# Two pairs of weight pieces in flight, three normalisations on GpSimd, and a new order, in a four-layer transformer kernel

## The chip, the cores and the metric

The kernel runs on one core of a Trainium2 chip. The metric is device time in microseconds (us); lower is better. A core has five engines that run on their own and meet through semaphores: TensorE (PE, matrix products), VectorE (DVE, elementwise work), ScalarE (ACT, activations and copies), GpSimd (POOL, elementwise work at a slower pace) and SyncE (SP, which here only issues DMAs). DMAs move data between HBM, the on-chip memory SBUF and, as transposes, within SBUF. Products land in PSUM, which has 8 banks.

## What is computed

Four layers on x of 2048 tokens by 448, in bfloat16. Layers 0 and 2 are attention over a short dilated window, layers 1 and 3 are a gated product (here called FFN):

```
x = x + A(layernorm(x), wqkv, wo)          # layer 0
x = x + B(layernorm(x), w_gate, w_up, w_down)   # layer 1
x = x + A(layernorm(x), wqkv, wo)          # layer 2
x = x + B(layernorm(x), w_gate, w_up, w_down)   # layer 3

A: 16 heads of 28; each token looks at itself and the 7 tokens at distances 2, 4, ... 14 before it;
   logits = q.k * 28**-0.5, softmax over the 8 places, weighted sum of v, then times wo (448 x 448)
B: ((x @ w_gate) * (x @ w_up)) @ w_down     # 448 -> 1792 -> 448, no activation function
```

The same weights serve layers 0 and 2, and layers 1 and 3.

## The kernel before

**Tiling.** Tokens lie in 16 blocks of 128. A layer is worked in chunks of 256 or 512 tokens, named by layer and number: A00 to A04, B10 to B14, A20 to A23, B30 to B34. `SEQ` gives the order in which the chunks are described, and chunks of neighbouring layers overlap: B10 can run once the first blocks of layer 0 are finished. Nearly every product uses half of the 128 rows of the PE array, so two matmuls run side by side ("a pair").

**A block's way through attention.** `ln_chunk` makes the layer norm: bn_stats and bn_aggr on DVE (the rows with `st` and `mv`), two small ACT operations (`lnv`, `rstd`), and the normalisation proper, a `tensor_scalar` into `xn_sb` (L788), on DVE. In layer 0 the block is then transposed on PE (`Tps`, L798 and L802) and copied to `xnTa` (L809, L812) by ACT or DVE; later layers transpose by DMA (L791, issued by SP). `qk_chunk` makes queries and keys (products with `WQK`, copy to `qk` at L898), `v_group` the values (products with `WV`). Attention goes by nine groups of up to two query blocks. For a group, `attn_front` masks the queries (`Qz`, DVE, L1009), multiplies them with the keys in 64 small matmuls (S, L1021), takes the exponent on ACT (L1030) and applies the window mask on DVE (L1037); `attn_back` multiplies with the values in 64 small matmuls (AV, L1055), collects the result in `O_sb` (L1066, L1070), and `norm` divides by the softmax sum (L1080 to L1093). `y_blocks` multiplies by `wo_g` and adds into `x_sb` (L1110).

**FFN.** `b_chunk` has 14 units; a unit is seven pairs with `WGU` (gate and up weights side by side), a copy of the gate half by ACT (`g_sb`, L1146) and a product on DVE into `hT` (L1149). Four pieces of `WD` then make the output, in two parts: the first needs units 0 to 6, the second units 7 to 13.

**What sets the order.** All operations are handed to a list scheduler inside the kernel (`Sched`). It steps through a planned time with an estimate for each operation, takes on each engine the ready operation of lowest priority number, and writes the resulting fixed order for each engine. Priorities are the sum of a base, `PR` by kind, `JP` by chunk and `XP` by operation number; these tables hold tuned numbers. The small matmuls of S and AV ("bursts") are joined up to `JOIN` at a time, and a burst can take in the first steps of a waiting product, split into strips of 32 columns (L538, the "host"). The planner also models that PE's instructions arrive in lines: `LINE = 254` instructions, the first boundary moved by `LINE_0 = 62`; a line's delay is a constant by time (6.5, 5.5 or 3.9 us).

**Weights.** The input `x` and the attention weights are loaded first. Then SP issues, each step waiting for the one before to land: the four pieces of `wo_g`; the first pair (gate and up piece); and so on through six pairs (two halves of the columns, three parts of the rows, `KPARTS`), and the four pieces of `WD`, one at a time. So one pair is in flight. The write of ones into the scratch tensor `vt` stands behind `wo_g`. SP also issues the writes of value pieces to `vt` (L907), their transposed reads (L918), and the output; its queue is in order.

## Time and profile before

| | |
|---|---|
| time, median of 3 runs | 391.83 us (389.53 to 392.62) |
| profiled execution: its own time | 391.56 us |
| its span, first to last instruction | 389.6 us |
| PE busy | 380.8 us, 6565 matmuls |
| DVE busy | 287.0 us |
| ACT busy | 209.0 us |
| POOL busy | 7.8 us |
| TensorE clock granted, mean | 0.996 |

The page gives each engine's busy time and a row of 40 slices (9.74 us each) with tenths of busy time. PE looks full almost everywhere, but a busy PE is not PE at its peak: ends of matmuls are modelled, so short waits between matmuls vanish in that row. The starts are sharp, and the prediction goes by them. A group row reads: line, engine, operation, output and inputs, shapes, count, then busy us and mean ns of one, then idle time before them and what ended it. A timeline row reads: start, duration (both us), then the same, with the idle time and its releaser in brackets.

### The profile page before, as it was taken

How to read it: one execution, taken by the hardware profiler on the slowest of the kernel's cores; microseconds unless marked ns; L12 is line 12 of the kernel's file. 1: busy time of each engine (PE TensorE's matmuls, PEld its weight loads, DVE VectorE, ACT ScalarE, POOL GpSimd, SP SyncE). 2: the span in 40 equal slices, each digit the busy share in tenths (PEclk: the TensorE clock that was granted, in tenths of full speed). 3: DMA queues.
4: the chain of work that ended last, by engine and by line, in shares of the span. 5: the costliest groups of instructions: out<-in, count | busy, mean ns of one | idle time of the engine just before them, and what ended most of it. 6: DMA issues, size and time to landing. Idle time of an engine off the chain costs nothing.

```text
span 389.6 us, 14816 instructions
## 1 busy us (share of the span) xinstructions
PE 380.8 (98%) x6565; PEld 214.7 (55%) x6565; DVE 287.0 (74%) x638; ACT 209.0 (54%) x393; POOL 7.8 (2%) x37
## 2 busy tenths in 40 slices
PE   8989989899999999999999999999999999999997
PEld 3646558455555544454766557654555444544584
DVE  6998989599968975399656997575967994376343
ACT  4887865397455775246454455565634842263140
POOL 6010000000000000000000000000000000000000
PEclk9989999999999999999999999999999999999999
DMA  8543574710711313004113132310133042100201
GB/s 276 161 106 76 137 101 124 122 23 9 87 25 34 47 39 56 10 6 86 21 22 50 30 63 37 75 32 2 27 54 96 3 47 52 48 2 3 60 14 49
DMA packets 54867, 22.53 MB, mean 58 GB/s; under 512 B 44996, under 2 KB 54804, under 8 KB 54804
## 3 DMA queue, kind: packets, MB, share of 16 engines
q1 hardware_dynamic: 54372, 21.08, 27.4%
q8 instruction: 52, 0.85, 0.9%
q10 hardware_dynamic: 432, 0.52, 0.5%
q14 instruction: 11, 0.09, 0.1%
HBM read 8.54 MB, written 2.71 MB: 29 GB/s over the span
## 4 chain that ended last, share of the span: by engine, by line
PE 93%; ACT 3%; DMA 1%; issue 1%; DVE 1%; SPq 0%; ACTq 0%
PE ps L535 82%; PE ps L538 3%; PE ps L1055 2%; PE ps L1021 2%; PE ps L697 2%; ACT E_sb L1030 1%; PE ps L1161 1%; DMA WD<-in_B_w_down_dram 1%; ACT xnTa L812 1%; ACT qk L898 1%; ACT g_sb L1146 0%; ACT xnTa L809 0%; DVE x_sb L1110 0%; PE ps L802 0%; DVE hT L1149 0%
## 5 line engine op out<-in xcount | busy, mean ns | idle before, releaser
L535 PE MATMUL ps<-xnTb,WGU 64*128 64x512 bf16 (+1 forms) x1908 | 174.4, 332 | 0.2
L535 PEld LDWEIGHTS ps<-xnTb,WGU 64*128 64x128 bf16 x1908 | 92.6, 94 | 67.8 <-issue 1.1
L1146 ACT ACTIVATE g_sb<-ps 128x512 bf16<-128x512 f32 (+1 forms) x140 | 71.1, 511 | 87.8 <-PE ps L535 71.7
L1149 DVE TENSOR_TENSOR hT<-g_sb,ps 128x512 bf16<-128x512 bf16 (+1 forms) x140 | 79.6, 576 | 43.1 <-ACT g_sb L1146 40.7
L535 PE MATMUL ps<-WD,hT 64*128 64x448 bf16 x778 | 78.6, 349 | 1.5 <-DMA WD<-in_B_w_down_dram 1.4
L535 PEld LDWEIGHTS ps<-WD,hT 64*128 64x128 bf16 x778 | 36.9, 94 | 36.0 <-issue 1.7
L535 PE MATMUL ps<-xnTa,WQK 64*128 64x512 bf16 (+1 forms) x492 | 55.2, 360 | 0.5 <-ACT E_sb L1030 0.3
L1110 DVE TENSOR_TENSOR x_sb<-x_sb,ps 128x448 bf16<-128x448 bf16 x62 | 36.4, 615 | 23.3 <-PE ps L535 23.3
L1030 ACT ACTIVATE E_sb<-ps,shift_sb 128x1024 bf16<-128x1024 f32 (+1 forms) x36 | 36.8, 1073 | 24.5 <-PE ps L1021 24.4
L767 DVE BATCH_NORM_STATS2 st<-x_sb 128x6 f32<-128x448 bf16 x64 | 37.7, 612 | 0.2
L788 DVE TENSOR_SCALAR xn_sb<-x_sb,mv,rstd 128x896 bf16<-128x896 bf16 (+1 forms) x64 | 34.7, 568 | 2.7 <-ACT rstd L772 2.5
L535 PEld LDWEIGHTS ps<-xnTa,WQK 64*128 64x128 bf16 x492 | 23.9, 96 | 22.2 <-issue 1.5
L898 ACT ACTIVATE qk<-ps 128x1024 bf16<-128x1024 f32 (+1 forms) x26 | 24.6, 956 | 11.3 <-PE ps L535 11.2
L535 PE MATMUL ps<-wo_g,oT 64*128 64x448 bf16 x256 | 29.1, 349 | 0.1
L1037 DVE TENSOR_TENSOR E_sb<-E_sb,MK 128x1024 bf16<-128x1024 bf16 (+1 forms) x36 | 23.6, 661 | 6.8 <-ACT E_sb L1030 6.5
L1081 ACT ACTIVATE R_sb<-R_sb 128x480 f32<-128x480 f32 (+1 forms) x34 | 20.5, 603 | 11.1 <-DVE R_sb L1080 10.6
L535 PE MATMUL ps<-WV,xnTa 64*128 64x336 bf16 (+3 forms) x248 | 23.1, 304 | 0.0
L1080 DVE STREAM_SHUFFLE R_sb<-O_sb 128x480 f32<-128x480 f32 (+1 forms) x34 | 23.1, 696 | 0.0
L1093 DVE TENSOR_TENSOR oT<-O_sb,R_sb 128x480 bf16<-128x480 f32 (+3 forms) x36 | 22.0, 624 | 0.8 <-ACT R_sb L1082 0.6
L1009 DVE TENSOR_SCALAR Qz<-qk,qmask 128x960 bf16<-128x960 bf16 (+1 forms) x36 | 14.7, 451 | 9.2 <-PE ps L1021 8.0
L1082 ACT ACTIVATE R_sb<-R_sb 128x480 f32<-128x480 f32 (+1 forms) x34 | 20.0, 600 | 0.3
L535 PEld LDWEIGHTS ps<-wo_g,oT 64*128 64x128 bf16 x256 | 12.4, 94 | 12.4 <-DVE oT L1093 0.9
(64 smaller groups left out, 231.6 us busy)
## 6 DMA issues: line engine op xcount, KB each, us to landing
out_dram<-x_sb SPq DMA_DIRECT2D x15, 112.0 KB, 1.7
x_sb<-in_A_x_dram SPq DMA_DIRECT2D x3, 448.0 KB, 6.0
WGU<-in_B_w_gate_dram SPq DMA_DIRECT2D x4, 224.0 KB, 3.6
WGU<-in_B_w_up_dram SPq DMA_DIRECT2D x4, 224.0 KB, 3.9
WD<-in_B_w_down_dram SPq DMA_DIRECT2D x2, 448.0 KB, 4.0
WGU<-in_B_w_gate_dram SPq DMA_DIRECT2D x2, 336.0 KB, 4.5
WGU<-in_B_w_up_dram SPq DMA_DIRECT2D x2, 336.0 KB, 6.3
vt<-qk SPq DMA_DIRECT2D x42, 16.0 KB
```

The costliest lines, as they stand in the source:

```text
L535: return lambda E: E.matmul(out(), lhs(), rhs(), start=start, stop=stop)
L767: sc.add("dve", one(lambda E, B=B: E.bn_stats(st6[:, B, :], x_sb[:, B, :]), ("bn", li, B)), 525.0, deps=[("x", li - 1, B)] + ([("xn", li - ...
L788: sc.add("dve", one(lambda E, B=B, dst=dst, src=src: E.tensor_scalar(dst, src, mv[:, B, 0:1], rstd[:, B:B + 1], ALU.subtract, ALU.mult), ( ...
L898: return E.activation(dst, src, ACT.Copy) if hasattr(E, "activation") else E.tensor_copy(dst, src)
L1030: return E.activation(E_sb[:, slot, 2 * hp:2 * hp + 2, 0:w], ps[:, b0:b0 + 2, 0:w], ACT.Exp, bias=shift_sb[:, 0:1], scale=SCALE)
L1037: return E.tensor_tensor(e, e, MK[:, kind, 0:nc].unsqueeze(1).unsqueeze(1).to_broadcast([128, 2, w // nc, nc]), ALU.min)
L1080: sc.add("dve", one(lambda E: E.stream_shuffle(R_sb[:, rs, 0:w], O_sb[:, os_, 0:w], [DH] * 32), ("Rs", li, qb)), dve_est(w) + 20.0, deps=[ ...
L1081: sc.add("act", one(lambda E: E.activation(R_sb[:, rs, 0:w], R_sb[:, rs, 0:w], ACT.Ln), ("Rl", li, qb)), act_est(w, False), deps=[("Rs", l ...
L1093: return E.tensor_tensor(oT[:, :, a % HALF:a % HALF + z - a], O[:, :, a - tok:z - tok], R_sb[:, rs, 0:w].rearrange("p (h n) -> p h n", h=4 ...
L1110: sc.add("dve", one(lambda E: E.tensor_tensor(x_sb[:, B, :], x_sb[:, B, :], ps[:, bk[w], 0:D], ALU.add), ("x", li, B)), dve_est(D), deps=[ ...
L1146: sc.add("act", one(lambda E, gs=gs, bk=bk: E.activation(g_sb[:, gs, 0:nt], ps[:, bk[0], 0:nt], ACT.Copy), ("G", li, j, fc)), act_est(nt), ...
L1149: sc.add("dve", one(lambda E, gs=gs, bk=bk, fc=fc: E.tensor_tensor(hT[:, fc, hs, 0:nt], g_sb[:, gs, 0:nt], ps[:, bk[1], 0:nt], ALU.mult), ...
```

## The change

1. **Weight loads.** A list `gates` replaces the single gate. Each pair waits for the pair two steps back, so two pairs are in flight; the first two wait for parts of `x`. `wo_g` moves from ahead of the first pair to behind the first half (three pairs); the write of ones waits for a piece of the second half. The `WD` pieces wait two steps back as well. Each piece gets a semaphore of its own.
2. **Normalisation.** In layer 0 the planner may place the normalisation of blocks 3 to 9 on POOL, at a planned 2,250 ns; the planned DVE time in FFN layers goes from 540 to 645 ns.
3. **Planner.** The delay of an instruction line follows from the DMAs that are in flight (`line_at`) instead of constants; bursts are no longer joined (`JOIN` 3 to 1); caps, holds and all priority tables are new.
4. **The order that results.** On POOL the normalisations of blocks 3, 7 and 9 stand behind the mask building. On PE, all four first query-and-key units run ahead of the first values; five attention groups (before: four) and more of `wo` stand ahead of the first FFN product. All weight issues stand on SP ahead of the first write to `vt`. PE has 18 S and 18 AV bursts, each on its own, in 36 stretches (before: 33). The matmuls are the same, but for a few that are split into strips in other places (6559 instructions in place of 6565).

```
-JOIN = 3
+JOIN = 1
...
-HOLD_A = 5940.0
-HOLD_BA = 13780.0
-HOLD_BB = 680.0
-HOLD_N = 2
+HOLD_A = 12410.0
+HOLD_BA = 40320.0
+HOLD_BB = 12030.0
+HOLD_N = 1
...
-ATT_P = 3.0
+ATT_P = 1.0
 A_CAP = 5
-B_CAP = 6
+B_CAP = 8
...
+    def line_at(self, at):
+
+        t = at + self.LINE_A
+        for issued, landed in self.moves:
+            if issued <= at + self.LINE_B:
+                t = max(t, landed - self.LINE_B)
+        return t + self.LINE_C
...
-            self.lines.append(at + (self.LINE_H if at < self.HEAD_T else self.LINE_W if at < self.HEAD_W else self.LINE_T))
+            self.lines.append(self.line_at(at))
...
-    plain_dma("sp", ones_dst, ones_src, ("vones",), "d_one", deps=["c_ones"] + [("wo", j) for j in range(4)], lat=4000.0, prio=-44.5)
-    for j in range(4):
-        dst = wo_g[32 * j:32 * j + DH, :, :]
-        src = A_wo.rearrange("(c j e) d -> j e c d", c=4, j=4, e=DH)[j]
-        plain_dma("sp", dst, src, ("wo", j), "d_wo", deps=["c_wo", ("x", -1, 11)], lat=3600.0, prio=-45)
-    gate = [("wo", j) for j in range(4)]
+    plain_dma("sp", ones_dst, ones_src, ("vones",), "d_one", deps=["c_ones", ("wu", 1, 0)], lat=6000.0, prio=-44)
+    gates = [[("x", -1, 11)], [("x", -1, 15)]]
     for n in range(2):
         f0, f1 = F // 2 * n, F // 2 * (n + 1)
         for i, (a, z) in enumerate(KPARTS):
             for w, lo, src in (("wg", 0, B_w_gate), ("wu", 64, B_w_up)):
-                plain_dma("sp", WGU[lo:lo + 64, a:z, f0:f1], ..., f"d_{w}{n}", deps=gate, ..., mode=i)
-            gate = [("wg", n, i), ("wu", n, i)]
+                plain_dma("sp", WGU[lo:lo + 64, a:z, f0:f1], ..., f"d_{w}{n}{i}", deps=gates[-2], ..., est=650.0)
+            gates.append([("wg", n, i), ("wu", n, i)])
+        if n == 0:
+            for j in range(4):
...
+                plain_dma("sp", dst, src, ("wo", j), "d_wo", deps=["c_wo"] + gates[-2], lat=4000.0, prio=-44)
+            gates[-1] = gates[-1] + [("wo", j) for j in range(4)]
     for n in range(FC // 7 * 2):
         a, z = 7 * n // 2, 7 * (n + 1) // 2
-        plain_dma("sp", WD[:, a:z, :], ..., ("wd", n), f"d_wd{n // 2}", deps=gate, ..., mode=n % 2)
-        gate = [("wd", n)]
+        plain_dma("sp", WD[:, a:z, :], ..., ("wd", n), f"d_wd{n}", deps=gates[-2], lat=4200.0, prio=-44)
+        gates.append([("wd", n)])
...
-            sc.add("dve", one(lambda E, ...: E.tensor_scalar(dst, src, mv[:, B, 0:1], rstd[:, B:B + 1], ALU.subtract, ALU.mult), ("xn", li, B)),
-                   325.0 if par == 0 else 540.0, ...)
+            sc.add(("dve", "pool") if li == 0 and 3 <= B < 10 else "dve", one(lambda E, ...: E.tensor_scalar(...), ("xn", li, B)),
+                   {"dve": 325.0 if par == 0 else 645.0, "pool": 2250.0}, ...)
```

The tables `PR`, `JP`, `XP` and `HEAD_P`, which are new throughout, are left out.

More of the change, by code (lines that the diff above doesn't have):

```diff
@@ L36 @@
 HEAD_LN = 5
-HEAD_P = (-7243.45, -6839.28, 6873.65, 2231.18, -2220.8)
-HOLD_A = 5940.0
-HOLD_BA = 13780.0
-HOLD_BB = 680.0
-HOLD_N = 2
+HEAD_P = (-13350.35, -12608.87, 4149.99, 4834.42, -5790.0)
+HOLD_A = 12410.0
+HOLD_BA = 40320.0
+HOLD_BB = 12030.0
+HOLD_N = 1
 AV_EST = 288.0
@@ L58 @@
 NBK = 8
-PR = {'Qz': 1078.85, 'AV': -4851.85, 'rstd': -1339.07, 'bn': 4568.65, 'N': -1817.78, 'Gps': 8610.65, 'Tps': -31.38, 'H': -4889.6, 'S': 2643.48, 'VT': 544.99, 'Ex': 596.45, 'G': -2837.24, 'xn': -3500.95, 'QK': 2639.1, 'Ddps': 940.66, 'V': 567.07, 'x': -8.65, 'lnv': 5266.82, 'Oc': 2625.17, 'Oa': 3443.2, 'R': -727.31, 'VVps': -3592.23, 'Yps': -11164.33, 'PW': 3164.05, 'T': -1396.37, 'mv': -2211.6, 'Rs': 1799.38, 'Rl': -488.18, 'QKps': 1399.61, 'E': 778.94, 'wqk': 1537.92, 'wqp': 1028.96}
@@ L61 @@
-JP = {'A20': -25.69, 'B32': -196.33, 'B34': -5191.89, 'A22': -98.13, 'B13': 6648.45, 'A21': -2562.96, 'B12': 1135.93, 'A02': 1939.91, 'A03': 1924.97, 'B30': 4558.29, 'B31': -653.55, 'B10': -3350.57, 'B11': -1722.9, 'A23': -7569.63, 'A04': -2325.27, 'B33': 4017.0, 'A01': -2467.87, 'B14': -3725.84, 'A00': -900.45}
+PR = {'Qz': 4799.43, 'AV': -4782.7, 'rstd': -6066.81, 'bn': 10063.34, 'N': 913.74, 'Gps': 11694.76, 'Tps': -4880.31, 'H': -10872.83, 'S': 203.36, 'VT': 66.35, 'Ex': 2432.38, 'G': -8403.33, 'xn': -4241.77, 'QK': 746.33, 'Ddps': 1807.32, 'V': -1125.57, 'x': 232.06, 'lnv': 8673.99, 'Oc': 2256.02, 'Oa': 3868.14, 'R': -6136.18, 'VVps': -2694.46, 'Yps': -13771.91, 'PW': 5680.47, 'T': -1301.17, 'mv': -7586.23, 'Rs': 1454.22, 'Rl': 1876.37, 'QKps': 398.71, 'E': -1505.89, 'wqk': 3921.06, 'wqp': 1513.4}
@@ L62 @@
+JP = {'A20': 2129.71, 'B32': 145.71, 'B34': -8865.09, 'A22': -1908.07, 'B13': 6929.64, 'A21': -3873.02, 'B12': -320.7, 'A02': 4273.6, 'A03': 6346.7, 'B30': 6263.14, 'B31': 805.07, 'B10': -3539.76, 'B11': -146.0, 'A23': -11058.38, 'A04': -7082.55, 'B33': 8155.41, 'A01': -2596.71, 'B14': -5692.45, 'A00': 5097.12}
 LOAD_L = 2000.0
@@ L147 @@
     LINE_0 = 62
-    LINE_T = 3900.0
-    LINE_H = 6500.0
-    HEAD_T = 14000.0
-    LINE_W = 5500.0
-    HEAD_W = 46000.0
+    LINE_A = 1200.0
+    LINE_B = 1100.0
+    LINE_C = 2700.0
     def __init__(self):
@@ L276, in schedule @@
         self.pe_done = []
+        self.moves = []
         ndep, users = {}, {}
@@ L419, in schedule @@
                     free[e] = op.end
+                    if op.dma is not None:
+                        self.moves = self.moves[-39:] + [(op.end, max(op.end + op.lat, op.land))]
                 order[e].append((got, seq))
@@ L612, in build @@
     sem_names = ["pe", "act", "dve", "pool"]
-    sem_names += [f"d_x{i}" for i in range(NCH)] + ["d_stg0", "d_stg1", "d_stg2", "d_stg3", "d_wv", "d_wo", "d_wg0", "d_wg1", "d_wu0", "d_wu1", "d_wd0", "d_wd1", "d_out", "d_out2"]
+    sem_names += [f"d_x{i}" for i in range(NCH)] + ["d_stg0", "d_stg1", "d_stg2", "d_stg3", "d_wv", "d_wo", *[f"d_{w}{n}{i}" for w in ("wg", "wu") for n in range(2) for i in range(len(KPARTS))], *[f"d_wd{n}" for n in range(4)], "d_out", "d_out2"]
     sem_names += ["d_x0h"]
@@ L625, in act_table_load, with plain_dma @@
         return E.add_instruction(atl)
-    def plain_dma(q, dst, src, key, sem, deps=(), lat=LOAD_L, prio=0.0, tmin=None, mode=0):
-        sc.add(q, one(lambda E: E.dma_start(dst, src), key), {"sp": 520.0, "act": 500.0, "pool": 1000.0}[q], deps=deps, dma=sem, mode=mode, lat=lat, land=LAND.get(sem[2:], 0.0), prio=prio, tmin=tmin)
+    def plain_dma(q, dst, src, key, sem, deps=(), lat=LOAD_L, prio=0.0, tmin=None, est=None):
+        sc.add(q, one(lambda E: E.dma_start(dst, src), key), est or {"sp": 520.0, "act": 500.0, "pool": 1000.0}[q], deps=deps, dma=sem, mode=0, lat=lat, land=LAND.get(sem[2:], 0.0), prio=prio, tmin=tmin)
     CH_ROWS = [0, 128, 192, 320]
@@ L729, in build @@
             for w, lo, src in (("wg", 0, B_w_gate), ("wu", 64, B_w_up)):
-                plain_dma("sp", WGU[lo:lo + 64, a:z, f0:f1], src[64 * a:64 * z, f0:f1].rearrange("(k p) f -> p k f", p=64), (w, n, i), f"d_{w}{n}", deps=gate, lat=LOAD_L + 224 * (z - a) / RATE, prio=-44, mode=i)
-            gate = [("wg", n, i), ("wu", n, i)]
+                plain_dma("sp", WGU[lo:lo + 64, a:z, f0:f1], src[64 * a:64 * z, f0:f1].rearrange("(k p) f -> p k f", p=64), (w, n, i), f"d_{w}{n}{i}", deps=gates[-2], lat=1900.0 + 1000.0 * (z - a), prio=-44, est=650.0)
+            gates.append([("wg", n, i), ("wu", n, i)])
+        if n == 0:
+            for j in range(4):
+                dst = wo_g[32 * j:32 * j + DH, :, :]
+                src = A_wo.rearrange("(c j e) d -> j e c d", c=4, j=4, e=DH)[j]
+                plain_dma("sp", dst, src, ("wo", j), "d_wo", deps=["c_wo"] + gates[-2], lat=4000.0, prio=-44)
+            gates[-1] = gates[-1] + [("wo", j) for j in range(4)]
     for n in range(FC // 7 * 2):
         a, z = 7 * n // 2, 7 * (n + 1) // 2
-        plain_dma("sp", WD[:, a:z, :], B_w_down[128 * a:128 * z, :].rearrange("(c p) e -> p c e", p=128), ("wd", n), f"d_wd{n // 2}", deps=gate, lat=LOAD_L + 112 * (z - a) / RATE, prio=-44, mode=n % 2)
-        gate = [("wd", n)]
+        plain_dma("sp", WD[:, a:z, :], B_w_down[128 * a:128 * z, :].rearrange("(c p) e -> p c e", p=128), ("wd", n), f"d_wd{n}", deps=gates[-2], lat=4200.0, prio=-44)
+        gates.append([("wd", n)])
     WDR = [("wd", n) for n in range(4)]
@@ L787, in ln_chunk @@
             nt = 4 if par == 0 else 7
-            sc.add("dve", one(lambda E, B=B, dst=dst, src=src: E.tensor_scalar(dst, src, mv[:, B, 0:1], rstd[:, B:B + 1], ALU.subtract, ALU.mult), ("xn", li, B)),
-                   325.0 if par == 0 else 540.0, deps=[("rstd", li, B), ("mv", li, B), ("x", li - 1, B), prev], prio=prio - 0.2)
+            sc.add(("dve", "pool") if li == 0 and 3 <= B < 10 else "dve", one(lambda E, B=B, dst=dst, src=src: E.tensor_scalar(dst, src, mv[:, B, 0:1], rstd[:, B:B + 1], ALU.subtract, ALU.mult), ("xn", li, B)),
+                   {"dve": 325.0 if par == 0 else 645.0, "pool": 2250.0}, deps=[("rstd", li, B), ("mv", li, B), ("x", li - 1, B), prev], prio=prio - 0.2)
             if not by_pe:
```

2 lines of the change are left out of this document (1 added, 1 removed).

## The prediction

> **What bounds the kernel now.** First the busy row of the page, then stretches of 10 us, then the waits of PE.
>
> ```profile
> PE 380.8 (98%) x6565; PEld 214.7 (55%) x6565; DVE 287.0 (74%) x638; ACT 209.0 (54%) x393; POOL 7.8 (2%) x37
> ```
>
> PE is full. What its matmuls need at least follows from the starts in the timeline, where a stretch without a wait stands:
>
> ```profile
> 15.90 3.84 PE L535 MATMUL ps<-xnTa,WQK 64*128 64x512 bf16 x34
> ```
>
> 34 matmuls are 17 pairs; the last takes .16 beyond its start distance, so (3.84 - .16)/17 = .216 us a pair of 512 columns. Likewise .189 for 448, .143 for 336, .109 for 256. Summed over all matmuls this is **361.4 us**, for the new order too, since the products are the same. So 391.56 (the profiled execution) = 1.95 outside the span + 1.3 to the first matmul + 361.4 + 24.2 of lost time between + 2.8 behind the last. Only the 24.2 can move. I call the sum of prices ahead of a matmul its *position*, and the wall time less the position its *lag*. Before, the lag is 4.7 us at position 17.3, 7.4 at 18.6, 9.8 at 24.1, 13.4 at 42.2 (first FFN product, wall 55.6), 15.5 at 59.0 (wall 74.5), 25.5 at the end. So two thirds are lost in the first 75 us, where layer 0 starts:
>
> ```profile
> 20.00:30.00 10.00, 8.33 (x193) 4.90 (x191) 8.49 (x23) 8.43 (x18) 1.03 (x5) 0.83 0.46 111
> 40.00:50.00 10.00, 8.81 (x188) 4.45 (x182) 8.71 (x21) 8.52 (x14) 0.00 (x0) 1.00 0.63 124
> 90.00:100.00 10.00, 10.00 (x100) 4.64 (x96) 9.80 (x20) 5.76 (x11) 0.00 (x0) 1.00 0.06 13
> ```
>
> The columns are the stretch, its length, busy us of PE, weight loads, DVE, ACT, POOL, then the granted clock. In the first, the clock is .83: it was .5 for 3.41 us (26.64 to 30.05), after PE had lost .92, .79 and .48 us to DVE and ACT within 23.8 to 26.1. In both early rows DVE has 85% and more. Named stalls are few:
>
> ```profile
> PE ps L535 <- DMA WD<-in_B_w_down_dram: 1.4, 1, 1.4
> PE ps L1021 <- issue: 1.2, 1, 1.2
> ...
> 50.03 0.47 PE L1021 MATMUL ps<-Qz,qk 64*32 64x80 bf16 x38 [1.22 <-issue]
> 70.48 1.50 PE L535 MATMUL ps<-WD,hT 64*128 64x448 bf16 x14 [1.41 <-DMA WD<-in_B_w_down_dram]
> ```
>
> The first is the output weights, landed at 70.4, two us after the last `hT` of the first FFN chunk (68.43). The second is an instruction wait in the middle of an S burst. The instruction queue shows why:
>
> ```profile
> q8 instruction: 52, 0.85, 0.9%
> ...
> q8 instruction: 1, 0.02, 1.1%
> ```
>
> 52 packets of 16 KB serve 13,130 PE instructions, one per 252 (126 matmuls and their loads). Each leaves .2 to 4.0 us (mean 1.7) after PE passed the boundary before it, takes .9 to 1.45, and the waiting matmul started 1.6 us behind the packet's end. The second row is the stretch 43 to 50: PE passed the boundary at 43.24, the packet went at 47.2, in transfers that fill the queues, and the matmul ran at 50.03, **6.8 us** later. Unloaded it would be 1.7 + 1.15 + 1.6 = 4.5. A line covers 126 matmuls: some 13 us of wide products, but little more than 1 us of small ones.
>
> **The change, part by part.**
>
> *Weights two pairs at a time.* A pair took 4.65 us from issue to next issue (16.37, 21.03, 25.68), some 2 of them in transfer. All weights are 5.1 MB; with two in flight at 448 KB in 2 us they need 23 us, so the last `WD` piece lands near 38 in place of 70.4 if the first pair goes at 15. The 1.41 us wait at 70.48 (1.58 between the matmuls) goes. What is late next is the last `hT`, so the gain exists only if DVE gets there sooner. `wo_g` behind the first half must be there at its first product, position 30.1, about wall 42. All weight issues now stand on SP ahead of the first `vt` write, which went at 38.9 before; the last of them goes when the `WD` piece two back has landed, some 4 us before the end, at 34, so the writes behind it are not held (bounds 0 and +2, if the loads run a third slower). Gain: 0 to 1.6, inside the sum below.
>
> *Normalisation on POOL.* Three operations of .323 us (start to start) leave DVE, .97 in all. The trace has no such operation on POOL. Its rows there: a copy of 448 in 558 ns, a two-input product of 72 in 356 ns; by the first an operation costs .6 us, by the second, scaled by size, 2.5. I take the diff's 2.25, close to the upper row; POOL was idle for 14.1 us ahead of 22.77, so three in a row (6.75 us) hide there. Bounds: -1.0 us, and +1.3 if the last one is bare (2.25 - .97).
>
> *The order, to position 18.9.* Two of the three moved normalisations precede the waits at 23.8 to 26.1, which end on DVE: .65 off, lag 7.4 - .65 = 6.8, position 18.85 at 25.6. I leave out a half clock here.
>
> *Position 22.9 to 24.1.* From there to position 22.9 the lag grew by some .5 outside the half clock: wall 30.2. In the new order a line ends at 22.9 (in the fourth S burst) and the next at 24.0 (in the second AV burst): 1.1 us of streaming, while the smallest distance before was 1.4. The line called at 30.2 comes after 4.5 to 6.8 us, and at that time two weight pairs are under way. I take the middle, 5.6: position 24.05 at 35.8. PE is then idle 4.5 us, and the clock was .5 where a 3.41 us stretch had 35% of PE activity, and whole at 51%; a half clock that covers 1.2 us of the streaming behind costs .6 (bounds 0 and 1.7, the latter half of 3.41). Lag 12.4, against 9.8.
>
> *To the end of the first FFN chunk.* The new order has one more attention group ahead of the first FFN product (position 45.4, was 42.2). DVE's work from the same place to the last `hT` is, priced by start-to-start distances of its rows (.605 for an `hT` of 512, .32 of 256, .536 bn, .56 norm product, .588 shuffle, and so on), **35.9 us**. Before, from 33.8 to 68.43 it did 29.9 us of such work in 34.6: 86%. Part of its idle time was the instruction wait and PE's own lateness, which are paid already here, so I take midway to full, 93%: 38.6 us, and 35.8 + .6 + 38.6 = 75.0 for position 59.0. PE alone would be there sooner: 36.4 + 34.9 + 5 bursts of .35 (the rate of late bursts, below) = 73.0. The lag is 16.0, before 15.5: **+.5**. Both old stalls are gone, and the new line wait with the longer head gives it back.
>
> *The rest.* From position 59 the lag grew by 10.0, with 26 S and AV stretches at about .35 each as the main part. The new order has 26 there as well; FFN is fed by the same weights. Line boundaries stand 4.1 us apart or more, at the closest 3.0 before, which may save one late line of 1; more bursts stand alone, which may cost as much. I take 0, bounds -1 and +1.
>
> Sum: 391.56 + .5 = **392.1 us**, beside the median of 391.83.
>
> **Weighing a rule.** POOL beside DVE is what decides the second part. In the trace:
>
> ```profile
> 22.77 1.03 POOL L713 COPY WQK<-hT 128x64 bf16<-128x64 bf16 x5 [14.11 <-PE ps L535]
> ...
> 22.96 0.40 DVE L788 TENSOR_SCALAR xn_sb<-x_sb,mv,rstd 128x512 bf16<-128x512 bf16 x1
> ```
>
> The normalisation ran inside POOL's copies in .40 us, its usual 403 ns. So no block shows, though POOL's copies are short. The Trainium skill's page "SBUF — State Buffer", section "Who interferes with whom", says otherwise: DVE and GpSimd share a port pair, DVE's copies and `tensor_scalar` in their two-port modes take it whole, and the one who comes second fully blocks. The row here speaks against it as far as it reaches; the last rival below is what it would give.
>
> **Rivals.**
>
> 1. *The forecast*: gains and losses cancel, 392.1. Chance .45.
> 2. *The head packs tightly.* Fetches come at 4.5 us with no half clock (24.05 at 34.7) and DVE is full (35.9, 70.6); then PE's own 34.9 + 1.75 ends last, at 71.4, lag 12.4: -3.1, **388.4**. For it: weights done by 38 leave the queues empty in 40 to 70; against: DVE never ran at 100% in the head. A line in 3 us (the fastest delay, .2 + 1.15 + 1.6) gives 387. Chance .25, of which .15 beyond 1%.
> 3. *Slower by lines behind weights.* Two pairs in flight hold the call at 30.2 for 6.8 us (37.0), the idle PE brings the half clock (1.7), and DVE runs at 86% (41.7): 80.4, lag 21.4, +5.9: **397.5**. It decides from a delay of about 6.5 us. For it: the 6.8 of before stood in full transfers. Against: at most one pair may still be moving. Chance .17.
> 4. *Slower by POOL beside DVE.* If every copy, normalisation and two-input product of DVE that starts during POOL's 6.75 us waits for its end, some three quarters of DVE's work there, 5 us, come late; a little idle takes 1: **396**. Chance .08.
> 5. *The loads gain nothing*: two pairs share the transfers, the weights land no earlier, and the wait of 1.6 stays behind the last `hT`: 392.1 + 1.6 = **393.7**. Chance .05.
>
> About 1% (3.9 us) is what a measurement of this kernel tells from no change. Faster by more: .15 (out of 2). Slower by more: .28 (3, most of 4, and a tail of 1 and 5). Within: .57. The range runs from 387.2 (2 with a quick line) to 397.5 (3).
>
> **What will show it.** Right: no wait for `WD`; last `WD` landed before 45; a PE gap of some 4.5 us near matmul 600 (the second AV burst); three normalisations on POOL of about 2.2 us and DVE at its usual durations beside them; lag 14 to 16 at the first FFN chunk's end; 10 us of loss behind. Wrong: no gap at that line (2), a gap over 5.5 with .5 clock (3), DVE starts held until POOL's ends (4), or losses behind 75 us that are not 10, which I have only carried over.

## The result, and the profile after

The changed kernel takes **392.69 us** (median of 20 runs, 388.5 to 395.15), against 389.81 for the kernel before in the 20 runs beside it: 2.9 us or .7% between the medians. Over fast runs alone (within 1.5% of a kernel's fastest, which leaves out three of the changed kernel's) the ratio is 1.0044, 95% interval 1.0023 to 1.0065. Either way it is slower by less than the 1% that the prediction called no change, and the median is .6 us from the forecast of 392.1. The profiled execution took 390.99 (span 389.2, mean clock 1.000), which is .57 *less* than the profiled one before (391.56, mean clock .996). That the profile reads faster and the median slower turned out to be the key to the case.

The page's busy row:

```profile
PE 381.3 (98%) x6559; PEld 219.1 (56%) x6559; DVE 283.7 (73%) x631; ACT 208.0 (53%) x395; POOL 15.3 (4%) x42
```

Four stretches of the windows view (stretch, length, busy us of PE, weight loads, DVE, ACT, POOL, granted clock, DMA share, GB/s):

```profile
20.00:30.00 10.00, 9.04 (x243) 4.79 (x240) 9.08 (x26) 8.81 (x18) 3.46 (x7) 1.00 0.84 190
30.00:40.00 10.00, 7.65 (x186) 3.83 (x186) 6.06 (x14) 7.33 (x10) 0.00 (x0) 1.00 0.74 190
40.00:50.00 10.00, 9.96 (x292) 5.55 (x288) 9.91 (x22) 8.15 (x14) 0.00 (x0) 1.00 0.12 28
90.00:100.00 10.00, 10.00 (x244) 5.44 (x240) 7.76 (x16) 7.16 (x12) 0.00 (x0) 1.00 0.07 14
```

The kernel before, from 30 to 40:

```profile
30.00:40.00 10.00, 9.99 (x281) 6.07 (x278) 9.07 (x20) 8.01 (x14) 0.00 (x0) 1.00 0.34 88
```

PE lost time between 30 and 40, where before it was full, and gained some between 40 and 50. DVE is *idle* for four of the ten us from 30 to 40. The last but one column shows the loads: .74 and .84 of the DMA engines up to 40, .12 from 40 to 50, where it was .63 before. The waits of PE (us in all, times, longest):

```profile
PE ps L1066 <- issue: 2.3, 1, 2.3
PE ps L706 <- DVE eps_sb L667: 1.3, 1, 1.3
PE ps L813 <- DVE xnTa L823: 0.6, 2, 0.5
```

The timeline of PE around the worst of them, and at the first `WD` product:

```profile
31.26 0.68 PE L1032 MATMUL ps<-Qz,qk 64*32 64x64 bf16 x64
31.88 0.82 PE L544 MATMUL ps<-xnTa,WQK 64*128 64x512 bf16 x6
32.63 0.61 PE L1066 MATMUL ps<-E_sb,v_sb 64*32 64x64 bf16 x56
35.53 0.22 PE L1066 MATMUL ps<-E_sb,v_sb 64*32 64x64 bf16 x8 [2.29 <-issue]
...
72.03 1.49 PE L544 MATMUL ps<-WD,hT 64*128 64x448 bf16 x14
```

Eight matmuls before its end, the second pair of AV bursts stops for 2.3 us ("issue": the engine waits for nothing that the profile shows). PE had called the line (passed the boundary ahead of it) at 31.28; its 16 KB packet left at 33.1 and took 1.11 us; the matmul started 1.3 later. The first `WD` product at 72.03 has no wait in front of it any more.

The checkpoints, by the prediction's own measure (lag = wall time less the sum of prices ahead):

| position | before | forecast | after |
|---|---|---|---|
| 18.85 | 7.4 | 6.8 | 7.0 |
| 22.9 | 9.8 | 7.3 | 8.4 |
| 24.1 | 9.8 | 12.4 | 11.5 |
| 59.0 (first FFN chunk ends) | 15.5 | 16.0 | 15.2 |
| end | 25.5 | 26.0 | 25.2 |

### The profile page after: what moved, and what is told of

Its sections match the earlier page's. It is cut to its first block, busy times and chain, and to the rows that moved or that the text cites. A ratio compares the mean times of both kernels' runs of the same rounds, so it can differ in the third digit from the quotient of the medians.

```text
span 389.2 us, 14802 instructions
## 1 busy us (share of the span) xinstructions
PE 381.3 (98%) x6559; PEld 219.1 (56%) x6559; DVE 283.7 (73%) x631; ACT 208.0 (53%) x395; POOL 15.3 (4%) x42
## 4 chain that ended last, share of the span: by engine, by line
PE 91%; ACT 5%; DVE 3%; issue 1%
PE ps L544 80%; PE ps L547 3%; PE ps L706 2%; ACT E_sb L1041 2%; PE ps L1066 2%; PE ps L1032 2%; PE ps L1172 1%; DVE Qz L1020 1%; ACT qk L909 1%; DVE R_sb L1091 1%; ACT R_sb L1092 0%; ACT g_sb L1157 0%; DVE xn_sb L799 0%; ACT v_sb L1001 0%; DVE E_sb L1048 0%
## 5 line engine op out<-in xcount | busy, mean ns | idle before, releaser
L544 PEld LDWEIGHTS ps<-xnTb,WGU 64*128 64x128 bf16 x1908 | 94.3, 94 | 68.6 <-ACT g_sb L1157 1.7
L544 PE MATMUL ps<-WD,hT 64*128 64x448 bf16 x792 | 80.7, 349 | 0.0
L544 PEld LDWEIGHTS ps<-WD,hT 64*128 64x128 bf16 x792 | 39.4, 94 | 32.8
L544 PE MATMUL ps<-xnTa,WQK 64*128 64x512 bf16 (+1 forms) x494 | 55.8, 352 | 0.6 <-ACT E_sb L1041 0.3
L544 PEld LDWEIGHTS ps<-xnTa,WQK 64*128 64x128 bf16 x494 | 24.9, 94 | 20.3 <-ACT E_sb L1041 1.1
L909 ACT ACTIVATE qk<-ps 128x1024 bf16<-128x1024 f32 (+1 forms) x28 | 25.9, 931 | 19.5 <-PE ps L544 19.1
L1092 ACT ACTIVATE R_sb<-R_sb 128x480 f32<-128x480 f32 (+1 forms) x34 | 20.2, 602 | 5.3 <-DVE R_sb L1091 5.2
L1091 DVE STREAM_SHUFFLE R_sb<-O_sb 128x480 f32<-128x480 f32 (+1 forms) x34 | 22.9, 694 | 0.0
L1093 ACT ACTIVATE R_sb<-R_sb 128x480 f32<-128x480 f32 (+1 forms) x34 | 19.5, 597 | 0.2
L1077 ACT ACTIVATE O_sb<-ps 128x448 f32<-128x448 f32 (+3 forms) x27 | 13.9, 551 | 9.6 <-PE ps L1066 9.5
```

The lines of the kernel that those rows point to most:

```text
L544: return lambda E: E.matmul(out(), lhs(), rhs(), start=start, stop=stop)
L909: return E.activation(dst, src, ACT.Copy) if hasattr(E, "activation") else E.tensor_copy(dst, src)
L1091: sc.add("dve", one(lambda E: E.stream_shuffle(R_sb[:, rs, 0:w], O_sb[:, os_, 0:w], [DH] * 32), ("Rs", li, qb)), dve_est(w) + 20.0, deps=[ ...
L1092: sc.add("act", one(lambda E: E.activation(R_sb[:, rs, 0:w], R_sb[:, rs, 0:w], ACT.Ln), ("Rl", li, qb)), act_est(w, False), deps=[("Rs", l ...
```

## The experiments

Three theories of what the new time is made of: (1) the instruction line that is late in the AV burst, with the half clock that follows it in a part of the runs; (2) DVE, as the prediction had it, so that a wait of PE in the burst only replaces a wait a little later; (3) something else in the head. Eight kernels tell them apart. Four ran together with the kernel before at 389.68 us, four with it at 390.07. In the cuts of code below, the bodies of the helpers are left out and the comments are added.

### Lines moved by 84 matmuls

```
     sc.schedule()
+    # 12 of the warming matmuls (128x512): each becomes 8 of 32 columns
+    _shift(sc, warm, ps, wb, 12, 7, 8)
```

> The changed kernel, but 12 of the warming matmuls are each cut into 8 tiny ones (32 columns), so that every instruction line ends 84 matmuls earlier and the two that ended 1.1 us apart (second AV burst) now stand at least 3 us from each other in the head; order, loads and engines as in the changed kernel. Theory 1 (the line stall there, 2.3 us in the profile, and the half clock that its idle PE brings in a part of the runs are what the changed kernel loses): median 389.5, down about 3 us from 392.69, the wait in the AV burst gone, granted clock 1.000 in most runs. Theory 2 (DVE sets the end of the first FFN chunk, as the forecast had it, and PE only waits there instead of here): 392, down .5 or less, lag at the first FFN chunk's end still 15 us or more. Theory 3 (the half clock comes from something else in the head): down 2.3, the clock below 1 in half of the runs as before.

Measured: **389.29 us** (388.94 to 391.18, 12 runs), 3.4 under the changed kernel and the same as the kernel before (ratio .9999, .9983 to 1.0015). The timeline of PE, same place:

```profile
30.68 0.68 PE L1047 MATMUL ps<-Qz,qk 64*32 64x64 bf16 x64
31.29 0.82 PE L544 MATMUL ps<-xnTa,WQK 64*128 64x512 bf16 x6
32.04 0.68 PE L1081 MATMUL ps<-E_sb,v_sb 64*32 64x64 bf16 x64
32.66 0.61 PE L544 MATMUL ps<-xnTa,WQK 64*128 64x512 bf16 x4
```

All 64 AV matmuls run in one piece. Matmul for matmul, this trace is .6 us ahead of the changed kernel's before the burst and 3.0 ahead behind it, so the wait was worth 2.4 there; and it is *still* 3.02 ahead at the end of the first FFN chunk and at 220 us. Nothing else was waiting behind that line: theory 2 falls. (Between 220 and 270 us it gives 1.1 back; .69 of that is a wait for `v_sb`, the values that come by DMA transposes.) The granted clock was 1.000 in all 12 runs, so theory 3 falls too. Runs at clock 1.000 alone take 389.50 in the mean here and 390.57 in the changed kernel, so about 1.1 of the 3.4 us is what the wait itself costs (1.9 are left at the end of this trace); the rest goes with the half clock.

### The control: lines moved by one whole line

```
-    _shift(sc, warm, ps, wb, 12, 7, 8)
+    _shift(sc, warm, ps, wb, 14, 9, 8)   # 126 more matmuls: one line
```

> A control for the shifted lines: 14 warming matmuls cut into 10 tiny ones each, 126 more matmuls, which is one instruction line (127 with its loads), so that all later lines end within one matmul of where they end in the changed kernel; the warming is changed as much as in the run with 84. Theory 1 (the place of the lines is what the 84 changed): the wait in the second AV burst is back with 2 to 2.5 us, the granted clock is below 1 in half of the runs, median 392 to 393. Rival (the changed warming itself gained the 3 us): 389 to 390, no matter where the lines end.

Measured: **393.99 us** (389.75 to 394.95, 12 runs; ratio to the kernel before 1.0072, 1.0036 to 1.0108), above the 392 to 393 expected. The wait is back, and the clock is below 1 in 7 of the 12:

```profile
32.20 0.63 PE L1081 MATMUL ps<-E_sb,v_sb 64*32 64x64 bf16 x58
35.06 0.22 PE L1081 MATMUL ps<-E_sb,v_sb 64*32 64x64 bf16 x6 [2.23 <-issue]
```

So it is the place of the lines that was worth 3.4 us in the median, and not the warming.

### Normalisations back on DVE, in two kernels

```
+    # ("xn", 0, B) for B in 3, 7, 9: from POOL's order into DVE's, by planned start
+    _move(sc, "pool", "dve", [("xn", 0, B) for B in (3, 7, 9)])
```

In the changed kernel:

> The changed kernel with the three normalisations (blocks 3, 7, 9) back on DVE at the place where POOL had begun them; all else in its order. Theory 1 (POOL takes .97 us of DVE work off a path that DVE sets): +.6 to +1.0. Theory 2 (DVE waits for PE's line at 31 to 35 anyway, so the work is hidden): within .3 of 392.69. Theory 3 (POOL beside DVE costs more than it takes away): -.5 to -2.

Measured: **393.00 us** (390.88 to 393.61, 6 runs), .3 from the changed kernel; at clock .995 and .996 it is 393.11 against 392.89. The longest wait of PE in its timeline:

```profile
35.90 0.22 PE L1077 MATMUL ps<-E_sb,v_sb 64*32 64x64 bf16 x7 [2.85 <-issue]
```

Two stretches of its windows view:

```profile
30.00:37.00 7.00, 3.72 (x150) 1.95 (x148) 2.20 (x5) 4.39 (x5) 0.00 (x0) 1.00 0.80 181
37.00:40.40 3.40, 3.40 (x22) 1.25 (x20) 2.42 (x7) 2.53 (x4) 0.00 (x0) 0.50 0.69 216
```

This profile caught what the changed kernel's did not: after 2.85 us without a line, the clock is .50 from 37.00 to 40.41. In those 3.4 us PE starts 22 matmuls, where the changed kernel's profile, undisturbed, has 36 in the same stretch. Matmul for matmul this trace loses .57 us in the wait and 1.69 in the half clock, and keeps both to the end (2.16 behind). Why the wait is longer here, no run shows.

With the lines moved, where no wait covers DVE:

> The run with the lines shifted by 84, with the three normalisations back on DVE. With the line wait gone nothing covers them any more. Theory 1 (DVE sets the head then, so POOL is worth its .97): 390.0 to 390.4 against 389.3. Theory 2 (PE alone sets the head, DVE has room): within .3 of 389.3.

Measured: **389.34 us** (388.87 to 390.95, 12 runs) beside 389.29 without. The .97 us of work that POOL takes over are worth nothing measurable, covered or not: PE sets the head here, and DVE has room.

### Normalisations on POOL, in the kernel before

```
+    # blocks 3, 9, 7: from DVE's order to POOL, ahead of its WQK copies
+    _move(sc, "dve", "pool", [("xn", 0, B) for B in (3, 9, 7)], ...)
```

> The kernel before with the normalisations of blocks 3, 9 and 7 on POOL, ahead of its WQK copies; all else in its order. Theory 1 (DVE sets the waits at 23.8 to 26.1): -.6 to -1.0 of 389.8, and less half clock behind them. Theory 2 (the 2.1 us of POOL are late for the transposes of blocks 7 and 9, whose order is fixed): +.5 to +2. Theory 3 (hidden): within .3.

Measured: **391.26 us** (390.58 to 392.30, 11 runs), ratio 1.0040 (1.0020 to 1.0060). POOL and PE in its timeline:

```profile
22.29 2.08 POOL L799 TENSOR_SCALAR xn_sb<-x_sb,mv,rstd 128x512 bf16<-128x512 bf16 x1 [2.06 <-ACT rstd L783]
...
24.42 0.42 PE L813 MATMUL ps<-ident,xn_sb 64*128 64x64 bf16 x16 [0.97 <-POOL xn_sb L799]
```

The first of its waits of PE:

```profile
PE ps L813 <- POOL xn_sb L799: 2.3, 2, 1.3
```

Theory 2 of this run: an operation of 2.08 us in place of .40 is late for its transposes when the order around it stays. The normalisations on POOL need the new order to be harmless; they were not what made it fast or slow.

### The loads alone, in the kernel before

```
+    # SP: weight issues as the changed kernel has them, all ahead of the first vt write,
+    # each pair waiting for the pair two back, a semaphore for each piece
+    _loads(sc)
```

> The kernel before with the changed kernel's weight loads alone: two pairs in flight, first pair behind x, wo_g behind the first half, all weight issues ahead of the first vt write; orders of PE, DVE, ACT and POOL as before. Theory 1 (the forecast's terms): the WD wait of 1.4 goes and the instruction wait of 1.2 in the S burst at 48.5 goes too, since the queues are empty by 43: 2.6 less, 387.2 against 389.8. Theory 2 (what is late next than WD is the last hT, and only the WD wait partly goes): 0 to -1. Theory 3 (the earlier weight transfers hold up instruction lines and the first transposes in 15 to 38): +1 to +3.

Measured: **389.08 us** (387.40 to 391.11, 12 runs), ratio .9992 (.9970 to 1.0013). In its trace PE is .4 to .9 us later than before on the way to 48 us, .72 there; the line wait in the S burst there is gone (.92 gained by the first FFN product), the `WD` wait too (1.41 gained at the first `WD` product), and 1.41 are left at the end. Its own wait list:

```profile
PE ps L1050 <- issue: 0.8, 1, 0.8
PE ps L831 <- DVE WQK L742: 0.7, 1, 0.7
PE ps L1050 <- ACT xnTa L841: 0.6, 1, 0.6
```

The .8 is a line wait in an S burst at 26.66, while the weights move, where none had been. So both gains of theory 1 are there and theory 3 takes a part back. The median shows .6, within its uncertainty; runs of equal granted clock show .9 (1.000: 388.26 against 389.15; .996: 389.22 against 390.15), but these are 3 and 7 runs of this kernel.

### The same, lines moved by 28

```
+    _loads(sc)
+    _shift(sc, warm, ps, wb, 4, 7, 8)
```

> The kernel before with the two-pair loads, and with its lines 28 matmuls earlier (4 warming matmuls cut into 8), by which the smallest distance of two lines in the head grows from 1.4 to 3.1 us. If the waits called issue (1.2 before, .8 with the loads alone) are lines, they go: 388.2 to 388.6 against 389.1. If the half clock there comes from PE's waits on DVE and ACT at 24 to 26, the granted clock stays below 1 in two thirds of the runs. Rival (those waits have another cause): 389.1, same waits.

Measured: **388.85 us** (387.70 to 391.83, 12 runs), ratio .9976 (.9954 to .9998): the best of all, 1.2 us under the kernel before and, by the medians, 3.8 under the changed one, if a little above the 388.2 to 388.6 expected. The line wait of .8 is gone, and the list starts, behind the first matmul's, with waits for DVE and ACT:

```profile
PE ps L845 <- DVE WQK L756: 0.7, 1, 0.7
PE ps L1064 <- ACT xnTa L855: 0.6, 1, 0.6
```

Those are the waits of the old order, and the granted clock is below 1 in 6 of 12 runs, where two thirds were expected.

### The last weights held back, in the changed kernel

```
+    for k in (("wg", 1, 2), ("wu", 1, 2)):
+        sc.ready[k][0].deps.append(("AV", 0, 2))
+    for n in range(4):
+        sc.ready[("wd", n)][0].deps = [("AV", 0, 2)]
```

> The changed kernel with the last gate and up pair and the four pieces of WD held back until the second pair of AV bursts is through (wall 35.7), all five then in flight at once; the rest as it is. So the queues should be empty when PE calls for the line at 31.3. Theory 1 (the line waits behind weights): the packet leaves .5 to 1.1 us after the call, as the ones called later do, and not 1.8 to 2.6; the wait in the AV burst falls from 2.3 to about 1.2, half clocks become fewer, median 390.5 to 391.5. Rival A (the delay of a line is its own): the wait stays 2.0 or more, 392.7. Rival B (the late weights are missed, by vt or by the first WD product): the gain in the burst comes back as a wait at 52 or 72.

Measured: **390.46 us** (389.42 to 392.03, 12 runs; ratio to the kernel before 1.0012, .9992 to 1.0032). PE in its timeline, at the burst and later:

```profile
31.73 0.62 PE L1073 MATMUL ps<-E_sb,v_sb 64*32 64x64 bf16 x56
33.46 0.22 PE L1073 MATMUL ps<-E_sb,v_sb 64*32 64x64 bf16 x8 [1.12 <-issue]
...
46.31 0.61 PE L544 MATMUL ps<-xnTa,WQK 64*128 64x256 bf16 x8 [0.71 <-issue]
...
51.19 0.45 PE L1073 MATMUL ps<-E_sb,v_sb 64*32 64x64 bf16 x37 [0.36 <-issue]
...
55.12 0.28 PE L544 MATMUL ps<-xnTa,WQK 64*128 64x256 bf16 x2 [0.58 <-issue]
```

The transfers explain it. The DMA row of the changed kernel from 31.3 to 32.9, ahead of its packet, and that of this kernel from 30.4 to 33.4, with it (40 slices each, tenths of the 16 DMA engines):

```profile
DMA  9929979999899999899999999999999979999999
```

```profile
DMA  6563000007000000000000000000000000000000
...
q8 instruction: 1, 0.02, 1.9%
```

With full queues the packet left 1.8 us after the call at 31.28; with empty ones .7 after the call at 30.37, and the wait fell from 2.29 to 1.12. Theory 1 holds for the line. Rival B came true as well, in its own way: the held weights now delay the lines called at 39.69 (packet at 43.7, 4.0 later) and after, and three new waits (.71, .36 and .58) eat the gain. Weights are not all that can hold a packet: the line called at 46.31 left at 48.92, 2.6 us later, while the DMA engines were busy for 14% of the time. What held that one stays open. At full clock the two kernels take the same: 390.46 (11 runs) and 390.57 (8 runs). What the hold removed from the median, 2.2 us, is the half clock.

### What the runs' clock shows

| kernel | wait for a line in the head, us | runs with mean clock below .9985 | mean us at clock 1.000 | mean us at .995 and .996 |
|---|---|---|---|---|
| before (63 runs beside the eight) | 1.2 | 36 of 63 | 389.77 | 390.29 |
| before, loads alone | .8 | 9 of 12 | 388.26 | 389.22 |
| before, loads, lines moved by 28 | none over .2 | 6 of 12 | 388.54 | 389.61 |
| before, xn on POOL | .9 | 4 of 11 | 390.90 | 391.90 |
| changed | 2.3 | 11 of 20 | 390.57 | 392.89 |
| control, one whole line | 2.2 | 7 of 12 | 390.37 | 394.41 |
| changed, xn on DVE | 2.9 | 5 of 6 | 390.88 | 393.11 |
| changed, weights held | 1.1 | 0 of 12 | 390.46 | |
| changed, lines moved by 84 | none | 0 of 12 | 389.50 | |
| the same, xn on DVE | .5 | 0 of 12 | 389.52 | |

A window of 3.41 us at half clock in a run of 390 lowers the mean to .9956, which is the .995 or .996 of these runs; .991, which some have, is two of them.

The kernel before has the window as often as the changed one. What differs is its price: .5 us between the last two columns before, 1.0 to 1.1 in the three kernels made from it, and 2.2 to 4.0 in the changed kernel, its control and the one with xn on DVE. At clock 1.000 the changed kernel is .8 slower than the kernel before, at .995 and .996 it is 2.6 slower, though the two rows were not measured side by side. The 1.69 seen in a trace is not all of the 2.3, nor of the control's 4.0 (3 runs); where the rest goes, no profile shows.

## Why the prediction was right

**The total** was right by .6 us and the range held it, but the closeness is in part luck. The sum starts from a profiled run of 391.56 with a half clock in it, while the kernel before took 389.81 in the 20 runs beside; the rise was forecast as .5 us and is 2.9 between the medians (.44% by the ratio, 1.7 us). Its main claim, that the gains (the `WD` wait, the S-burst line) are given back by one new line wait in the second AV burst, is what the runs show. Step by step:

- *Weights two pairs at a time.* Right in the main. The `WD` wait is gone, the last piece, issued at 37.5, is there at 41.3 (forecast 38), and the loads alone are worth .6 us in the median and .9 at equal clock, inside the forecast's 0 to 1.6.
- *Normalisation on POOL.* The price of 2.25 us was right (2.07 to 2.32). The gain of .97 was an upper bound, and the .65 that I took from it for the stretch before 18.9 is not there: moving the work back cost nothing with or without the line wait. The lag at 18.85 came out near the forecast (7.0 for 6.8) by luck: with the normalisations back on DVE it is 6.4 there.
- *The line at 22.9.* The place was right to the burst. The sizes were off in opposite directions: PE came there at 31.3 and not 30.2, and the line took 4.3 us and not 5.6, so position 24.1 was at 35.6, for 35.8 forecast without the half clock: luck again. The 1.1 us of streaming between the two lines took 2.0, so PE waited 2.3 us and not 4.5.
- *The half clock.* Taken as .6 us for every run; it is nothing in some runs and 1.7 or more in the others. That is why the profiled run (390.99, clock 1.000) lies below its forecast and the median (392.69) just above.
- *To the end of the first FFN chunk.* **This step failed.** I let DVE's 35.9 us of work at 93% end the stretch, at 75.0, with PE alone at 73.0. It ended at 74.1, and what set it was PE: 2.4 us saved in the burst were still 2.4 at the end, and .97 us more on DVE changed nothing. PE's own price was the term that was too small, by half: I added 1.75 us to the prices of its matmuls, and the lag rises by 3.6 from 24.1 to 59.0. The five stretches of small matmuls, .35 each in my sum, do cost .26 to .38 each, 1.7 in all. The other 1.8 us are lost in the wide products between them, which the sum put at nothing. The 10.0 us carried over behind position 59 were right (10.0).

Of the rivals, 2 (a tight head) comes nearest to the kernel with its lines moved, 389.3 for 388.4 priced, though there PE waits for no line at all. Rival 3 (the line behind weights, with a half clock) was the right mechanism: the weights cost the line about 1.1 us, not 2.3, and the half clock comes in about half of the runs. Rival 5 falls with the `WD` wait. Rival 4, which the prediction's rule on POOL and DVE leads to, is answered below.

What stays open: with lines moved, the new order is level with the old one although the loads in it are worth .6 to .9, so the rest of it seems to cost about as much. The longer head (3.6 us of lag between 24.1 and 59.0, where before had 2.9 besides its two named stalls) would fit; no run isolates it.

## What to carry to other kernels

Where instructions are small, count them: a line that PE runs through in 2.0 us can't hide a fetch of 4.3 us, and moving the boundary by 84 tiny matmuls of no account was worth more in the changed kernel (3.4 us in the median) than the loads (.6 to .9) and the new home of three operations (nothing) together. A wait on the busiest engine has to be priced with what the clock does behind it, in each run and not on average; one profile shows one of the cases. And a stall that is taken away tells what was behind it: here the gain went unshortened through the next 190 us, so nothing else was waiting behind that line there; 1.1 of it was lost later.

## What the runs showed of the hardware

- **An instruction line waits for weights.** In the changed kernel the packets of the lines called up to 35.6 left 1.8 to 2.6 us after the call, while weights moved; those called at 41.8, 51.9, 55.8, 64.6 and 79.3 left .5 to 1.1 after. I had priced it so; for the line in the AV burst the held weights show that it is the transfers (1.8 against .7). The 2.6 us of the held kernel's line at 46.31 show that it is not always them.
- **The half clock needs no idle window of its length.** In the kernels with a wait of 2.2 to 2.9 us in the AV burst it came in 23 of 38 runs, in the one with 1.1 in none of 12; but in the kernel before it came in 36 of 63, and its profile shows it behind three waits of .92, .79 and .48 within 2.3 us. So no single wait decides. The Trainium skill's page "TensorE: Matmul & The Clock Gate", section "What's actually happening", gives a free-running window of 3413 ns and a throttle after one idle window. The length agrees (.50 for 3.41 us), and a free-running window fits that only a part of the runs is hit; but no wait here reached 3.4 us, so a window that is idle in part is enough. How much can be estimated from the positions: over the 3.41 us just ahead of the half clock PE had streamed for .35 of the time in the kernel before, .34 with the loads alone, .27 with these and the lines moved, and .30 with xn on DVE, where the 3.41 us ahead of those had .40 and the clock stayed whole. With lines moved by 84 no stretch of that length after the first 10 us of the profile is under .5, and with the weights held the lowest is .35. That puts the limit, as an estimate, near .35 to .40.
- **DVE is slowed beside POOL, not blocked.** The changed kernel's timeline, POOL's first normalisation and DVE beside it:

```profile
10.78 2.08 POOL L799 TENSOR_SCALAR xn_sb<-x_sb,mv,rstd 128x512 bf16<-128x512 bf16 x1 [1.69 <-ACT rstd L783]
...
11.05 0.63 DVE L799 TENSOR_SCALAR xn_sb<-x_sb,mv,rstd 128x512 bf16<-128x512 bf16 x1
11.60 0.61 DVE L778 BATCH_NORM_STATS2 st<-x_sb 128x6 f32<-128x448 bf16 x1
...
12.22 0.78 DVE L799 TENSOR_SCALAR xn_sb<-x_sb,mv,rstd 128x512 bf16<-128x512 bf16 x1
```

  The same operation takes .40 us alone. Over the kernels with POOL normalisations, the 24 that started inside one took .53 in the median and .78 at most; bn_stats beside them kept its .61. The Trainium skill's page "SBUF — State Buffer", section "Who interferes with whom", has it that the second of the two fully blocks. A DVE operation that starts at 11.05 and is done at 11.68, inside a POOL operation that ends at 12.86, was not blocked; it lost .23. The rule is right that only some operations suffer. It is too strong in how much, unless this operation runs outside the two-port modes that the page speaks of, which no run shows.
